# A recurrence and an MLP in one kernel: the first step's scores issued at once, ScalarE's weight passes ordered one by one, new orders of the work

## The chip, the cores and the metric

The kernel runs on one core of one Trainium2 chip. The metric is the device time of one execution in microseconds; the time before is the median of three runs.

## The reference

Two blocks are computed one after the other, in float32. The first is a gated linear recurrence over 768 positions for 4 x 8 heads of width 48; the second is a two-layer network with a PReLU between its layers, applied to the 3072 rows of 384 that the first one gives.

```python
# q, k, v, f_logit: (4, 8, 768, 48)
f = 1.0 / (1.0 + np.exp(-f_logit))
for t in range(S):
    state = f[:, :, t, :, None] * state + np.einsum('bhd,bhe->bhde', k[:, :, t], v[:, :, t])
    y[:, :, t] = np.einsum('bhd,bhde->bhe', q[:, :, t], state)
x = y.transpose(0, 2, 1, 3).reshape(B * S, H * D)          # 3072 x 384
h = x @ w_in                                               # w_in: 384 x 2048
g = np.maximum(h, 0.0) + alpha * np.minimum(h, 0.0)
out = g @ w_out                                            # w_out: 2048 x 384
```

## The kernel before

The work is cut into twelve steps: a step is a pair of batches (`bp`, 0 or 1; `u` counts the two batches in it) and a chunk of 128 positions (`c`, 0 to 5). Each step goes through four stages, each a Python generator that yields between its parts:

- `prepare` loads f, q, k and v, takes the sigmoid on ScalarE (f), copies q into `qd` and multiplies it into three lagged copies on VectorE (L275), makes running products (`ps`, `ss`, L305, L307), and from these the scaled queries `us` and `q3` and the scaled keys `k4`, `ks`, `kh`. In the first chunk of a pair of batches it also makes `k16` and `q16` (L375, L392). Its last part copies q3 into the matrix `A` on ScalarE (L407) and, for later chunks, moves the transposed keys into `ksn` by sixteen small DMAs on SP's queue (L415).
- `carry` makes the scores between blocks (`off`, L432; for the first chunk also the k16 products, L442), which ScalarE copies into `ad` (L446) and `A` (L450). For a first chunk it transposes the keys on TensorE (`pk`, L459) and ScalarE copies them to `ksn` (L462). Then it makes the products of keys and values (`pd`, L472) and moves the state on into `vs` (`moved`, L482 to L488).
- `attend` makes the scores inside blocks: `raw` from k and the lagged q (L508), `qu` from k4 and us (L523), which VectorE copies under masks into `ad` (L514; L545 in a first chunk, L529 in others), ScalarE copies `ad` into `A` (L551), TensorE multiplies by vs (`py`, L562), ScalarE copies that out (`y`, L571), and DMAs from three queues turn it into `xT` (L591). In the first step TensorE does this instead (`xt`, L580).
- `network` multiplies xT by w_in in eight tiles (`ph`, L606), ScalarE and VectorE apply the PReLU (`neg` L611, `gate` L613), and TensorE multiplies by w_out: plainly in the first step (`po`, L626), by a seven-product scheme in the others (`pa` to `pe`, L645, with sums `S` of the gates, L687, and `u2`, `o` on VectorE).

The weights come in sixteen pieces of 64-bit words. A piece is fetched into a `raw` buffer by SP (L196), ScalarE makes three passes over it (`pos` L201, `neg` L203, the low part L204) and VectorE two (`lead` L214, `both` L219). The halves of w_out are then combined on VectorE (`W`, L706).

PSUM has eight banks: four as two double banks (`pair`, for raw, qu, off, pk, pd, py) and four single ones (`bank`, for ph, po, pa to pe, xt, idle). TensorE, VectorE and ScalarE take their instructions in the order in which the program issues them, and that order is written out by hand: one string per step, in which a letter runs a stage to its next yield and a number repeats it. P and Q are `prepare` of this step and of the next, O is `carry`, S `attend`, n `network` of the step before, a and b the ScalarE passes on w_in and w_out, w and v the VectorE passes on them, W the sums of w_out.

```python
first = (
    "P5 a w P a2 O w S w a w a2 S Q S O S w Q2 S Q2 S w",
    "a2 w b w O w n2 b2 v S P v2 n2 S b v Q n b n O S2 v n b v n Q2 b v Q b n S v2 W Q W S n2 W n W",
    ...
)
usual = "S n2 O P n S Q n2 Q n3 O n S2 n Q S Q2 S n3"
```

POOL's and SP's queues are ordered by the planner of the framework. Ahead of the first step 56 small idle products run on TensorE.

Of the kernel before, what the change touches and what calls it, by code (L numbers as in the profile page):

```python
# [8 lines left out]
F32 = mybir.dt.float32  # L9
I16 = mybir.dt.int16  # L10
# [14 lines left out]
NB = DB // 4  # L25
WP = 768
IDLE = 56
RAWS, TOPS, LEADS = 4, 3, 4


@with_exitstack
def kernel(
# [62 lines left out]
    def pair(name):  # L95
        return psa.tile([128, 2, 512], F32, tag="pair", name=name)
# [71 lines left out]
    def load_weights(dst, src, name):  # L168

        rows_ = NK if dst is w_in_sb else 1  # L180
        pieces_ = dst.shape[1] * dst.shape[2] // WP
        if rows_ == 1:
            dst = dst.rearrange("p a n -> p (a n)").unsqueeze(1)
        width = WP // rows_
        words = src.rearrange("p (a n) -> p a n", a=rows_).bitcast(I16)
        got = {}

        def of(n):
            return dst[:, :, n * width:(n + 1) * width]

        def by_row(t):
            return t.rearrange("p (a n) -> p a n", a=rows_)

        def upper(n):
            raw = stage.tile([128, WP, 4], I16, tag="raw", name=f"{name}_raw{n}", bufs=RAWS)
            nc.sync.dma_start(out=raw.rearrange("p (a n) four -> p a (n four)", a=rows_)[:, :, 0:4 * width - 1],  # L196
                              in_=words[:, :, 4 * n * width + 1:4 * (n + 1) * width])

            top = raw[:, :, 2]
            pos = stage.tile([128, WP], I16, tag="pos", name=f"{name}_pos{n}", bufs=TOPS)  # L200
            nc.scalar.activation(pos, top, AF.Relu, bias=bias[:, 0:1], scale=8.0)  # L201
            neg = stage.tile([128, WP], I16, tag="wneg", name=f"{name}_neg{n}", bufs=TOPS)
            nc.scalar.activation(neg, top.bitcast(U16), AF.Relu, bias=bias[:, 1:2], scale=8.0)  # L203
            nc.scalar.activation(as_int(n, I32), by_row(raw.bitcast(U32)[:, :, 0]), AF.Copy, scale=2.0 ** -13)  # L204
            got[n] = raw, pos, neg

        def as_int(n, dtype):
            t = of(n).bitcast(dtype)
            return t if dtype is I32 else t.rearrange("p a (n two) -> p a n two", two=2)[:, :, :, 1]

        def lead(n):
            raw, pos, neg = got.pop(n)
            t = stage.tile([128, WP], BF16, tag="lead", name=f"{name}_lead{n}", bufs=LEADS)
            nc.vector.tensor_tensor(t, pos.bitcast(BF16), neg.bitcast(BF16), ALU.subtract)  # L214
            got[n] = t

        def both(n):
            t = by_row(got.pop(n).bitcast(I16))
            nc.vector.tensor_tensor(as_int(n, I16), as_int(n, I16), t, ALU.add)  # L219

        def uppers():
            for n in range(pieces_):
                upper(n)
                yield

        def rests():
            for n in range(pieces_ + 1):
                if n < pieces_:
                    lead(n)
                if n:  # L230
                    both(n - 1)
                yield

        return uppers(), rests()

    def rows(par):
        return slice(64 * par, 64 * par + D)
# [182 lines left out]
    def carry(bp, c, x):  # L420

        i = f"{bp}_{c}"
        q3, ks, kh, f64 = (x[n] for n in ("q3", "ks", "kh", "f64"))
        off = pair(f"off_{i}")
        for u in range(U):
            for hp in range(HP):
                for cc in range(NC2):
                    g = (u * HP + hp) * NC2 + cc
                    o = (u * HP + hp) * DB
                    for par in range(2):  # L430
                        r_ = rows(par)
                        nc.tensor.matmul(off[CH * cc:CH * cc + DB, par, o:o + DB],  # L432
                                         lhsT=kh[r_, g], rhs=q3[r_, g, 2], start=True, stop=True)
        if not c:
            for u in range(U):
                for hp in range(HP):
                    for j in range(NJ):
                        g = (u * HP + hp) * NJ + j
                        o = U * HP * DB + (u * HP + hp) * 16
                        for par in range(2):  # L440
                            r_ = rows(par)
                            nc.tensor.matmul(off[DB * j:DB * (j + 1), par, o:o + 16], lhsT=x["k16"][r_, g],  # L442
                                             rhs=x["q16"][r_, g], start=True, stop=True)
            for u in range(U):
                o = U * HP * DB + u * HP * 16
                nc.scalar.copy(ad[:, u, :, :, 16:DB], off[:, :, o:o + HP * 16].rearrange("p r (h t) -> p r h t", h=HP))  # L446
        for cc in range(NC2):
            s_ = slice(CH * cc, CH * cc + DB)
            for par in range(2):
                nc.scalar.copy(A[s_, :, par * HP:(par + 1) * HP, CH * cc + DB:CH * (cc + 1)],  # L450
                               off[s_, par, 0:U * HP * DB].rearrange("p (u h t) -> p u h t", u=U, h=HP))


        if not c:
            pk = pair(f"pk_{i}")
            for u in range(U):
                for hp in range(HP):
                    a = (u * HP + hp) * NC2
                    nc.tensor.transpose(pk[:, u, hp * 128:(hp + 1) * 128], ks[:, a:a + 2].rearrange("p c s t -> p (c s t)"), ident)  # L459
            ksn = x["ksn"] = work.tile([128, U, HP * 128], F32, tag="ksn", name=f"ksn_{i}", bufs=1)  # L460
            for u in range(U):
                nc.scalar.copy(ksn[:, u], pk[:, u])  # L462
        yield
        pd = pair(f"pd_{i}")
        ksn = x["ksn"]
# [28 lines left out]
    def attend(bp, c, x):  # L494

        i = f"{bp}_{c}"
        k, k4, us = (x[n] for n in ("k", "k4", "us"))


        QL, QS = (UW, UW) if c else (VW, C)  # L500
        for u in range(U):
            raw = pair(f"raw{u}_{i}")
            for hp in range(HP):
                for j in range(NJ):
                    g = (u * HP + hp) * NJ + j
                    for par in range(2):
                        r_ = rows(par)
                        nc.tensor.matmul(raw[DB * j:DB * (j + 1), par, hp * C:hp * C + QW],  # L508
                                         lhsT=k[r_, g * DB:(g + 1) * DB], rhs=qd[r_, g], start=True, stop=True)
            adu = ad[:, u].rearrange("p r h (i t) -> p (r h) i t", t=4)  # L510
            rv = raw.rearrange("p r (h x) -> p (r h) x", h=HP)
            for d in range(4):
                n = 4 - d
                nc.vector.copy_predicated(  # L514
                    adu[:, :, :, d:4], mraw[:, d, :, d:4].bitcast(I32).unsqueeze(1).broadcast_to((128, H, NB, n)),
                    rv[:, :, QO[d]:QO[d] + NB * n].rearrange("p h (i t) -> p h i t", t=n))
            qu = pair(f"qu{u}_{i}")
            for hp in range(HP):
                for j in range(NJ):
                    g = (u * HP + hp) * NJ + j  # L520
                    for par in range(2):
                        r_ = rows(par)
                        nc.tensor.matmul(qu[DB * j:DB * (j + 1), par, hp * QS + 4:hp * QS + QL],  # L523
                                         lhsT=k4[r_, g * DB:(g + 1) * DB], rhs=us[r_, g, 4:QL], start=True, stop=True)
            if c:
                for m in range(1, NB):
                    lo = UO[m] + (4 if m == 1 else 0)
# [5 lines left out]
            else:  # L533
                qv = qu.rearrange("p r (h x) -> p (r h) x", h=HP)
                adh = ad[:, u].rearrange("p r h (a t) -> p (r h) a t", a=2)
                for m in range(1, NQ):
# [5 lines left out]
                    if m > 1:  # L542
                        to = adh[:, :, :, 4 * m:16]
                        of, by = (t.rearrange("p h (a t) -> p h a t", a=2) for t in (of, by))
                    nc.vector.copy_predicated(to, by, of)  # L545
            yield

        for u in range(U):
            for j in range(NJ):
# [139 lines left out]
    def halves_of_w_out():  # L689
# [12 lines left out]
        for to, x_, y_, op in ((t3, b22, b12, ALU.subtract), (t2, t3, b11, ALU.add), (t4, t2, b21, ALU.subtract),  # L702
                               (b12, b12, b11, ALU.subtract)):
            for h in range(2):
# [3 lines left out]

    idle = bank("idle")

    steps = [(bp, c) for c in range(NC) for bp in range(B // U)]
    first = (
        "P5 a w P a2 O w S w a w a2 S Q S O S w Q2 S Q2 S w",
        "a2 w b w O w n2 b2 v S P v2 n2 S b v Q n b n O S2 v n b v n Q2 b v Q b n S v2 W Q W S n2 W n W",
        "n S P n2 S n W n O Q n3 O S Q n S Q n Q S2 Q n3",
        "S n3 P S Q S n O n O n4 Q S Q S Q n S Q n3",
    )
    usual = "S n2 O P n S Q n2 Q n3 O n S2 n Q S Q2 S n3"
    pieces = {key: part for keys, parts in (("aw", load_weights(w_in_sb, w_in, "w_in")),
                                            ("bv", load_weights(w_out_sb, w_out, "w_out")))  # L720
              for key, part in zip(keys, parts)}

    pieces["W"] = halves_of_w_out()

    def begin(n):
        if n >= len(steps):
# [72 lines left out]
```

## Time and profile before

| | |
|---|---|
| median of three runs | 626.85 us (626.29 to 627.31) |
| the profiled execution, its own time | 627.25 us |
| its span, first to last instruction | 625.4 us |
| TensorE busy | 590.1 us, 94% |
| VectorE busy | 502.5 us, 80% |
| ScalarE busy | 265.3 us, 42% |
| ph, the largest group on TensorE | 260.3 us, 1152 instructions |

A float32 product shows as two MATMUL instructions. PE is TensorE, PEld its weight load, DVE VectorE, ACT ScalarE, POOL GpSimd, SP SyncE; a q behind an engine's name is its DMA queue. L508 is line 508 of the kernel. A share of busy time is an average over the whole span; the stages at the start have other limits than the rest.

### The profile page before, as it was taken

What the parts mean: (1) busy time and instruction counts of PE and PEld (TensorE: products, weight loads), DVE (VectorE), ACT (ScalarE), POOL (GpSimd) and SP (SyncE); (2) the same over time, 40 slices, a digit from 0 to 9 for tenths busy, and PEclk for the clock granted to TensorE, in tenths of its full rate; (3) what the DMA queues carried; (4) which work ended last, traced back from release to release, by engine and by line L of the source; (5) the groups of instructions that cost most, each with busy time, mean ns of one, the idle gap of its engine ahead of it and who ended that gap; (6) DMA issues with size and microseconds to landing.
All of it is one profiled execution on the core that took longest, in us unless ns stands there. A gap on an engine that the chain in (4) does not pass through costs nothing.

```text
span 625.4 us, 19119 instructions
## 1 busy us (share of the span) xinstructions
PE 590.1 (94%) x8220; PEld 525.8 (84%) x8220; DVE 502.5 (80%) x1013; ACT 265.3 (42%) x482; POOL 60.5 (10%) x119
## 2 busy tenths in 40 slices
PE   3458999999999999999999999999999999999997
PEld 3346876789899889889889889889889889889997
DVE  7599889999799599699699699699799789663261
ACT  5797893361442542442443343353253253222110
POOL 8020001001001001001001001001001000000000
PEclk9996999999999999999999999999999999999999
DMA  9766514313414313313313223223222310300100
GB/s 314 261 229 191 176 60 95 77 35 87 85 36 91 78 37 86 65 57 85 58 64 85 54 69 85 53 69 77 59 71 68 70 37 12 66 4 12 41 0 26
DMA packets 68116, 50.43 MB, mean 81 GB/s; under 512 B 47168, under 2 KB 60608, under 8 KB 68032
## 3 DMA queue, kind: packets, MB, share of 16 engines
q1 hardware_dynamic: 56656, 25.01, 15.4%
q0 software_dynamic: 6864, 22.35, 12.7%
q10 hardware_dynamic: 4512, 1.85, 1.4%
q8 instruction: 65, 1.06, 0.7%
q14 instruction: 19, 0.16, 0.1%
HBM read 36.21 MB, written 4.72 MB: 65 GB/s over the span
## 4 chain that ended last, share of the span: by engine, by line
PE 70%; DVE 19%; ACT 8%; issue 1%; DMA 1%; ACTq 0%; DVEq 0%
PE ph L606 37%; PE pa L645 8%; PE pc L645 7%; PE pb L645 4%; PE qu L523 3%; PE pe L645 2%; PE pd L645 2%; DVE us L318 2%; PE raw L508 2%; PE py L562 1%; PE pd L472 1%; DVE q L356 1%; DVE us L309 1%; DVE k L335 1%; DVE vs L486 1%
## 5 line engine op out<-in xcount | busy, mean ns | idle before, releaser
L606 PE MATMUL ph<-xT,w_in_sb 128*128 128x256 f32 x1152 | 260.3, 384 | 0.1
L606 PEld LDWEIGHTS ph<-xT,w_in_sb 128*128 128x128 f32 x1152 | 217.6, 191 | 32.9 <-issue 2.6
L611 ACT ACTIVATE neg<-ph 128x512 f32<-128x512 f32 x96 | 57.2, 597 | 200.8 <-PE ph L606 154.1
L613 DVE SCALAR_TENSOR_TENSOR gate<-neg,om,ph 128x256 f32<-128x256 f32 x192 | 82.0, 477 | 59.7 <-ACT neg L611 59.6
L645 PE MATMUL pa<-w_out_sb,gate 128*128 128x192 f32 x352 | 63.4, 333 | 0.0
L645 PE MATMUL pc<-t,S 128*128 128x192 f32 x352 | 60.9, 326 | 0.0
L645 PEld LDWEIGHTS pa<-w_out_sb,gate 128*128 128x128 f32 x352 | 56.7, 190 | 2.1 <-DVE gate L613 0.6
L645 PEld LDWEIGHTS pc<-t,S 128*128 128x128 f32 x352 | 57.8, 190 | 0.1
L514 DVE COPY_PREDICATED ad<-mraw,raw 128x256 f32<-128x256 int32 (+1 forms) x96 | 42.4, 442 | 8.3 <-PE raw L508 5.8
L529 DVE COPY_PREDICATED ad<-mquad,qu 128x224 f32<-128x224 int32 (+6 forms) x140 | 41.9, 300 | 6.2
L551 ACT COPY A<-ad 32x256 f32<-32x256 f32 x96 | 38.6, 402 | 1.4
L571 ACT COPY y<-py 128x512 f32<-128x512 f32 x24 | 12.9, 592 | 58.1 <-PE py L562 58.1
L318 DVE TENSOR_TENSOR us<-us,fs 128x768 f32<-128x768 f32 (+5 forms) x60 | 37.0, 616 | 0.3
L302 ACT COPY us<-qd 128x256 f32<-128x256 f32 x48 | 29.8, 675 | 7.6 <-DVE qd L275 7.5
L687 DVE TENSOR_TENSOR S<-gate 128x512 f32<-128x512 f32 x44 | 30.3, 688 | 0.8
L645 PE MATMUL pb<-t,gate 128*128 128x192 f32 x176 | 30.4, 326 | 0.0
L645 PE MATMUL pe<-w_out_sb,S 128*128 128x192 f32 x176 | 30.4, 326 | 0.0
L645 PE MATMUL pd<-w_out_sb,S 128*128 128x192 f32 x176 | 30.4, 326 | 0.0
L508 PEld LDWEIGHTS raw<-qd,k 48*32 48x32 f32 x1536 | 18.3, 109 | 14.3 <-issue 8.7
L508 PE MATMUL raw<-qd,k 48*32 48x80 f32 x1536 | 23.3, 243 | 7.1 <-ACT A L450 5.2
L407 ACT COPY A<-q 48x512 f32<-48x512 f32 x44 | 27.1, 617 | 6.7 <-DVE q L356 6.1
L562 PEld LDWEIGHTS py<-A,vs 128*64 128x64 f32 x768 | 24.8, 144 | 5.8 <-issue 2.2
(109 smaller groups left out, 743.8 us busy)
## 6 DMA issues: line engine op xcount, KB each, us to landing
w_out_raw<-in_w_out SPq DMA_DIRECT2D x8, 767.8 KB, 4.5
w_in_raw<-in_w_in SPq DMA_DIRECT2D x8, 767.2 KB, 8.3
q<-in_qT POOLq DMA_DIRECT2D x11, 512.0 KB, 4.1
f<-in_fT POOLq DMA_DIRECT2D x11, 512.0 KB, 4.1
k<-in_kT POOLq DMA_DIRECT2D x11, 512.0 KB, 4.5
out<-o SPq DMA_DIRECT2D x24, 192.0 KB, 2.1
vs<-in_v POOLq DMA_DIRECT2D x22, 192.0 KB, 3.5
ksn<-kt SPq DMA_DIRECT2D x80, 32.0 KB, 2.0
```

The source lines that it names most:

```text
L302: nc.scalar.copy(q4[:, :, :, r], qdv[r][:, :, :, 0])
L318: nc.vector.tensor_tensor(us[:, :, UO[m]:UO[m] + 4 * n].rearrange("p g (i r) -> p g i r", r=4), us[:, :, skip:skip + 4 * n].rearrange("p g ...
L508: nc.tensor.matmul(raw[DB * j:DB * (j + 1), par, hp * C:hp * C + QW], lhsT=k[r_, g * DB:(g + 1) * DB], rhs=qd[r_, g], start=True, stop=True)
L514: nc.vector.copy_predicated(adu[:, :, :, d:4], mraw[:, d, :, d:4].bitcast(I32).unsqueeze(1).broadcast_to((128, H, NB, n)), rv[:, :, QO[d]: ...
L529: nc.vector.copy_predicated(ad[:, u, :, :, 4 * m:DB], mquad[:, lo:lo + n].bitcast(I32).unsqueeze(1).unsqueeze(1).broadcast_to((128, 2, HP, ...
L551: nc.scalar.copy(A[s_, u, :, s_], ad[s_, u].rearrange("p r h t -> p (r h) t"))
L562: nc.tensor.matmul(py[64 * par:64 * par + 64, u, o:o + CH], lhsT=vs[bp][:, cc, u, hd * D:hd * D + 64], rhs=A[:, u, par * HP + hp, CH * cc: ...
L606: nc.tensor.matmul(ph[:, j * T:(j + 1) * T], lhsT=w_in_sb[:, kt, m * 128:(m + 1) * 128], rhs=xT[:, kt], start=(kt == 0 and j == 0), stop=( ...
L611: nc.scalar.activation(neg, phv, AF.Relu, scale=-1.0)
L613: nc.vector.scalar_tensor_tensor(gate[:, m % NH, m // NH], neg[:, j], om[:, m:m + 1], phv[:, j], ALU.mult, ALU.add)
L645: nc.tensor.matmul(to[:, 0:DH], lhsT=of(f), rhs=by(f), start=(f == 0 and not more), stop=(f == NH - 1), skip_group_check=True)
L687: nc.vector.tensor_tensor(to, x_, y_, op)
```

## The change

Five things are changed. Three raw buffers hold the fetched pieces of weights instead of four. Each of ScalarE's three passes over a piece is now a part of its own in the order, w_in's and w_out's in one line ("a"), and the next piece is fetched after the third pass of the one whose buffer it takes. In the first step, `attend` issues the raw scores of both batches at once, before the rest of `prepare`, then both batches' masked copies and qu; `off` and `pk` of that step take single banks, and a yield divides `carry` there. In all first chunks the k16 products and their copies (four instead of two) come before those of `off`. Seven idle products of 128x256 ("J") are put into the first step's order, and all orders are new.

```diff
-RAWS, TOPS, LEADS = 4, 3, 4
+RAWS, TOPS, LEADS = 3, 3, 4
...
-        def upper(n):
-            raw = stage.tile([128, WP, 4], I16, tag="raw", ..., bufs=RAWS)
+        def fetch(n):
+            raw = raws[n] = stage.tile([128, WP, 4], I16, tag="raw", ..., bufs=RAWS)
             nc.sync.dma_start(...)
+        def upper(n):
+            top = raws[n][:, :, 2]
             pos = stage.tile(...)
             nc.scalar.activation(pos, top, AF.Relu, bias=bias[:, 0:1], scale=8.0)
+            yield
             neg = stage.tile(...)
             nc.scalar.activation(neg, top.bitcast(U16), AF.Relu, bias=bias[:, 1:2], scale=8.0)
-            nc.scalar.activation(as_int(n, I32), by_row(raw.bitcast(U32)[:, :, 0]), AF.Copy, scale=2.0 ** -13)
-            got[n] = raw, pos, neg
+            got[n] = pos, neg
+            yield
+            low = raws.pop(n).bitcast(U32)[:, :, 0]
+            nc.scalar.activation(as_int(n, I32), by_row(low), AF.Copy, scale=2.0 ** -13)
...
-        off = pair(f"off_{i}")
-        ... off products (moved behind the k16 products)
+        plain = (bp, c) == steps[0]
+        def two(name):
+            if plain:
+                return [bank(f"{name}{n}_{i}") for n in range(2)]
+            t = pair(f"{name}_{i}")
+            return [t[:, n] for n in range(2)]
+        off = two("off")
         if not c:
             ... k16 products
             for u in range(U):
-                nc.scalar.copy(ad[:, u, :, :, 16:DB], off[:, :, o:o + HP * 16]...)
+                for par in range(2):
+                    nc.scalar.copy(ad[:, u, par, :, 16:DB], off[par][:, o:o + HP * 16]...)
+        ... off products
         ... copies of off into A
+        if plain:
+            yield
         if not c:
-            pk = pair(f"pk_{i}")
+            if plain:
+                spare.clear()
+            pk = two("pk")
...
+        if (bp, c) == steps[0]:
+            raws = [scores(u) for u in range(U)]
+            yield
+            qus = []
+            for u in range(U):
+                within(u, raws[u])
+                qus.append(quad_scores(u))
+            yield
+            for u in range(U):
+                between(u, qus[u])
+            yield
+        else:
+            for u in range(U):
+                within(u, scores(u))
+                between(u, quad_scores(u))
+                yield
...
+    def kept_busy():
+        while True:
+            if not spare:
+                spare.append(bank("spare"))
+            nc.tensor.matmul(spare[0][:, 0:256], lhsT=ones[:, 0:128], rhs=ones[:, 0:256], start=True, stop=True)
+            yield
...
     first = (
-        "P5 a w P a2 O w S w a w a2 S Q S O S w Q2 S Q2 S w",
-        "a2 w b w O w n2 b2 v S P v2 n2 S b v Q n b n O S2 v n b v n Q2 b v Q b n S v2 W Q W S n2 W n W",
-        "n S P n2 S n W n O Q n3 O S Q n S Q n Q S2 Q n3",
-        "S n3 P S Q S n O n O n4 Q S Q S Q n S Q n3",
+        "P S P a P J a J2 P a J4 w a2 P w a P a O a O a S a3 w a S w S a2 Q S a3 O a S Q w a w Q S Q2",
+        "a2 w a3 n2 a O w v a4 S a2 v n S w P a3 v2 a S a n Q a v n S n O a2 n2 a v a Q a2 S Q v a4 v n v S W Q2 n2 Q W3 n",
+        "S n3 S n S n Q n W n O n S O n Q n S Q2 n S Q n2",
+        "S n P n O n S Q n3 S n Q n O S n Q n S Q2 S n Q n2",
     )
-    usual = "S n2 O P n S Q n2 Q n3 O n S2 n Q S Q2 S n3"
+    usual = "S n2 S n O n O n Q n3 Q n Q S3 n Q S n Q n Q n"
+    def uppers(parts):
+        for n in range(RAWS):
+            parts[n][0](parts[n][2])
+        for n, (_, upper, m) in enumerate(parts):
+            yield from upper(m)
+            if n + RAWS < len(parts):
+                fetch, _, ahead = parts[n + RAWS]
+                fetch(ahead)
+            yield
+    pieces = {"a": uppers(parts_in + parts_out), "w": in_rests, "v": out_rests}
+    pieces["J"] = kept_busy()
```

## The prediction

> **What bounds the kernel now.** I read the page first, then the busy time by stretch, then the timelines of ScalarE, TensorE, VectorE and the DMA queue. The page's first two parts (busy share; 40 slices, each 15.6 us):
>
> ```profile
> PE 590.1 (94%) x8220; PEld 525.8 (84%) x8220; DVE 502.5 (80%) x1013; ACT 265.3 (42%) x482; POOL 60.5 (10%) x119
> ...
> PE   3458999999999999999999999999999999999997
> ...
> ACT  5797893361442542442443343353253253222110
> ```
>
> PE is full from slice 5 on and idle for over half of slices 1 to 4, where ACT is nearly full. Busy time by stretch (PE, PEld, DVE, ACT, POOL, then clock and DMA):
>
> ```profile
> 20.00:27.70 7.70, 2.56 (x76) 2.12 (x66) 2.08 (x4) 7.66 (x14) 0.00 (x0) 1.00 0.69 197
> 27.70:38.00 10.30, 5.83 (x292) 4.99 (x293) 8.18 (x19) 10.24 (x14) 1.42 (x3) 1.00 0.72 231
> ...
> 46.00:58.00 12.00, 8.86 (x213) 7.32 (x214) 11.88 (x24) 8.05 (x13) 0.95 (x2) 0.71 0.52 147
> 58.00:66.00 8.00, 8.00 (x143) 6.60 (x145) 4.50 (x8) 5.64 (x13) 0.00 (x0) 0.79 0.59 193
> ```
>
> ACT sets 20 to 46 us, PE everything after 58. Of the 35.3 us that PE idles (625.4 - 590.1), 28 lie before 58 us; what is left is little. The timelines give the places (start, length, in brackets the idle time ahead and what ended it):
>
> ```profile
> 19.84 1.25 ACT L407 COPY A<-q 48x512 f32<-48x512 f32 x2 [6.06 <-DVE q L356]
> ...
> 45.60 1.07 ACT L571 COPY y<-py 128x512 f32<-128x512 f32 x2
> ```
> ```profile
> 27.77 1.34 PE L508 MATMUL raw<-qd,k 48*32 48x80 f32 x64 [5.22 <-ACT A L450]
> ...
> 46.82 4.51 PE L580 MATMUL xt<-y,dense 128*128 128x256 f32 x12 [2.00 <-ACT y L571]
> ...
> 55.95 1.97 PE L459 MATMUL pk<-ident,ks 128*128 128x128 f32 x8
> 57.71 7.17 PE L606 MATMUL ph<-xT,w_in_sb 128*128 128x256 f32 x24
> ...
> 119.48 1.07 PE L523 MATMUL qu<-us,k 48*32 48x112 f32 x64 [1.31 <-DVE ad L529]
> ```
> ```profile
> 251.98 1.08 PE L523 MATMUL qu<-us,k 48*32 48x112 f32 x64 [0.41 <-DVE vs L486]
> ```
> ```profile
> 110.69 3.56 DVE L706 TENSOR_TENSOR t<-t,w_out_sb 128x768 f32<-128x768 f32 x4
> 114.27 0.87 DVE L613 SCALAR_TENSOR_TENSOR gate<-neg,om,ph 128x256 f32<-128x256 f32 x2
> ```
>
> Read: ACT once idles 6.06 us; the scores wait 5.22 us for ACT; the network (ph) starts at 57.7 though its input is ready at 51.7; VectorE finishes w_out's sums at 114.3, which costs PE 1.31 us; and a 0.4 us wait recurs in the later steps.
>
> **The change, part by part.** All terms are from this execution: 625.4 us of span, 627.25 us of its own time, 0.4 above the median 626.85 (626.29 to 627.31). I subtract what is gained from the median.
>
> *Scores at once.* With off and pk in four single banks, both double banks are free for raw0 and raw1. They follow the last lagged product (9.88 + 0.61 = 10.5 us) at 2 x 1.34 and are done by 13.2, not 32.9. The masked copies still wait for the copies of off into ad (L446), now at 23.1, and then take two L514 groups of 1.88, one w round of 1.42 (L214 and L219) and two L545 groups of 1.01: done at 30.4 instead of 37.9. By itself this brings nothing, since ACT's queue is the path. L446 becomes four copies instead of two: two took 0.31, a 128x64 copy 0.14 (L304), so +0.3.
>
> *Weight passes.* One piece takes 2.56 (pos 0.91, neg 0.87, low 0.78). Before L407 ACT now fits two pieces, not one. The second piece was issued near 4.6 and landed after 9.6, at 14.2, so ACT waits 0.4 for it. L407 comes 0.47 later (one L214 now stands before VectorE's last products): 20.3. So ACT's idle time goes from 6.1 to about 3.9. From 20.3 on its queue is: L407 1.26, pos 0.89, L446 0.56, L450 1.29, neg 0.88, ksn 0.95, low 0.79, a piece 2.56, pos 0.91, A 1.66, neg and low 1.66, f/kr/qd 2.57, A 1.66, a piece 2.56, vs 0.98, pos 0.91, us 2.28, neg 0.88: 25.3, so y starts at 45.6. That is the same as before: the idle time saved has gone into two more weight passes, the later L407 and L446. py (41.5 + 3.16) is ready by then. xT is ready near 51.7, as before.
>
> *Three buffers.* Pieces 3, 4, ... are fetched after low of 0, 1, ...: at 14, 17, 27 us, needed at 27, 29.5, 38. Landings took 4.2 to 16.8; 10.9 for the one nearest in time, which I take. At 16.8 piece 3 would cost 3.8. No other queue entry stands behind these fetches on SP until xT's at 97 us.
>
> *Idle products.* Seven of 128x256, each 0.45 (5.45/12) at best and 0.75 (4.51 x 2/12) as xt ran: 3.2 to 5.3 us in PE's empty stretch 13.2 to 19.5, ahead of the k16 products that wait for VectorE (L392). Cost nothing; with that cover gone they'd cost 3.2 to 5.3. Their gain: off, k16 and pk shorter (pk 1.97), but ACT, not PE, is what those copies wait for. Zero.
> Behind an idle stretch PE is slow here: the granted clock was 0.50 from 48 to 50 us, after PE had idled 2.0 us, and py took 3.16 at 41.7 where it takes 2.0 in full work. After this change PE idles from about 31 to 41 us, so I leave py and xt at their slow 3.16 and 4.51.
> [...]
>
> *ph first.* In step 1 the network's first two tiles now precede k16, off, pk. ph starts at 51.4, ends at 56.8 (5.45; if as slow as before, 7.17: 58.5). Then k16 1.3, off 0.7, pk 1.1 (half of 1.97): 60. ACT meanwhile: five passes to 56.0, two neg, one pass, L446, L450 to 60.2, ksn to 61.2. raw0 follows the first, qu0 the second, 0.7 each: ph2 starts at about 62.0; before, the third tile started at 66.24. PE is 4.2 ahead. But ACT now holds it: 20.5 us of queue (12 weight passes 10.4, L407 1.2, eight A copies 3.3, four neg 2.0, f/kr/qd 2.6, vs 1.0) end the vs copies at 81.7, and py waits for them, while PE is there at 62.0 + 18.5 (six tiles 16.1, scores 1.4, pd 0.9) = 80.5. So po ends at 81.7 + 2.0 + 20.8 = 104.5, not 107.4: 2.9.
> VectorE, from the last gates at 85.8 (after ACT's two passes and two neg, 2.7, behind vs): three w_out rounds 4.26, one L219 0.95, scans 1.32, L309/L335/L318 3.12, moved 2.14, the two product groups 3.7 and 4.4, W 5.45, in all 25.3: 111.1, 3.2 earlier than 114.27. qu1 of step 2 waits for the masked copies behind it (4.2, to 115.3), and PE is there at 104.5 + 10.5 = 115.0: the wait of 1.31 becomes 0.3. Start-up gain: 2.9 + 1.0 = 3.9. Bounds: 0.8 (slow ph and a late landing partly) to 5.
>
> *New usual order.* From 203.72 to 250.65 a step took 46.93; all eight from 156.36 to 536.23 took 379.87, 4.4 over 8 x 46.93. Named in the waits after 140 us: qu on L486 2.0 (five times 0.4), py on A 0.3. The moved pass (L482, L486) now comes before the last product group (4.4 us), so it ends some 5 us before the next scores: 2.3 goes. What is late next: py moves ahead of pc and pd, while eight A copies come after us and kept on ACT. From the end of ph7: neg 0.55, us 1.97, kept at 2.75, copies 3.33: 6.4 us; PE after pa and pb (5.3) and half of py (1.0) is there at 6.3. So 0.1 a step, 0.8 in all. Net 1.5; bounds 4.4 and -4.
>
> **Sum:** 3.9 + 1.5 = 5.4; 626.85 - 5.4 = 621.45 us.
>
> **Rivals.** (1) *Only the start-up counts:* py's wait for A takes what qu's wait gave (0.3 a step instead of 0.1), so the order gives -0.1 and the gain is 3.8 or less: about 623.3. For it: the tie at py is worked out from rows to 0.1 us. Against: even 0.3 needs a late us copy.
> (2) *Slower: pd waits for ksn.* In the usual order O moves from after ph7 to after ph3, 15 us after the step's start instead of 26, while its operand comes through 16 DMAs issued one by one on SP:
>
> ```profile
> 203.37 0.47 SPq L621 DMA_DIRECT2D out<-o  x1
> 203.88 1.25 SPq L415 DMA_DIRECT2D ksn<-kt  x2
> 205.24 0.53 SPq L621 DMA_DIRECT2D out<-o  x1
> 205.82 7.07 SPq L415 DMA_DIRECT2D ksn<-kt  x9
> ```
>
> 16 x 0.61 = 9.8 us, plus two stores (1.0) that wait for VectorE's last sums, plus 2.0 to 3.9 to land. The transpose ends 2 us before the step's start, so the last lands at 11 to 13: 2 us to spare. If SP starts only after the second store (at 1.5), it lands at 14 to 16; a further 2 us for a landing beside the 512 KB loads makes the wait 1.5 to 3. It decides above 5.4/8 = 0.7 us a step; at 1.6 us, eight steps cost 12.8, net 12.8 - 5.4 = 7.4: 634.3.
> (3) *No change:* a piece lands at 16.8 (3.8 us of ACT) and ph runs slow (1.7), together 5.5, which eats the 5.4: 626.9. Against: less is queued ahead of piece 3 than of the one that took 16.8.
>
> **How the numbers follow.** Forecast (gain 3 to 9) 0.60, rival 1 0.14, rival 3 0.06, rival 2 and its smaller forms 0.20. A measurement can tell about 0.2% (1.25 us): faster is below 625.6, slower above 628.1. Faster 0.74, same 0.06, slower 0.20. The forecast's own range is 617.8 to 624; with rivals 1 and 3 and the mild half of rival 2 the range is 617.8 to 629.
>
> **What would show it.** Right: raw0 and raw1 before 14 us; y near 45.6; ph from 51 to 52, ahead of k16; last W pass near 111; the qu waits on L486 gone; steps of about 47.05. Wrong: y or xT several us from 45.6 and 51.7; a wait of pd on ksn's DMAs; py waiting over 0.5 us for A; ACT idle before a weight pass.

## The result and the profile after

The changed kernel takes 630.98 us (median of 7 runs, 628.64 to 631.81), the kernel before 626.36 us on the same chip (624.88 to 627.31). The ratio is 1.0061, 95% interval [1.0046, 1.0076]: slower by 4.6 us, where 5.4 us of gain were predicted, and above the range (617.8 to 629.0). The profiled execution of after took 631.81 us with a span of 630.0 us, so it is the slowest of its seven; the numbers below are of this execution.

Busy shares and the 40 slices (15.75 us each) of the page of after:

```profile
PE 593.1 (94%) x8234; PEld 529.1 (84%) x8234; DVE 503.8 (80%) x1013; ACT 261.0 (41%) x486; POOL 62.6 (10%) x119
...
PE   7337899999999999999999999999999999999997
...
ACT  6398895362352244244244244244244244223110
```

ScalarE (ACT) was nearly full in slices 2 to 4 before and has a 3 in its second slice now, in which it mostly waits. Busy time by stretch for the place (PE, PEld, DVE, ACT, POOL, then clock, DMA share, GB/s):

```profile
20.00:24.00 4.00, 0.69 (x74) 0.59 (x64) 1.98 (x5) 2.21 (x3) 0.00 (x0) 0.92 0.99 322
24.00:28.00 4.00, 0.00 (x0) 0.00 (x0) 0.00 (x0) 0.00 (x0) 0.00 (x0) 0.50 0.92 194
```

From 24 to 28 us no engine does anything; only DMAs run. The timelines of TensorE and ScalarE say who waits for whom:

```profile
10.54 2.82 PE L519 MATMUL raw<-qd,k 48*32 48x80 f32 x128 [2.23 <-ACT us L301]
13.29 4.88 PE L753 MATMUL idle<-ones 128*128 128x256 f32 x14
19.71 0.99 PE L440 MATMUL off<-us 48*32 48x16 f32 x96 [1.53 <-DVE us L391]
29.32 0.44 PE L440 MATMUL off<-us 48*32 48x16 f32 x32 [8.63 <-issue]
```
```profile
20.32 1.25 ACT L406 COPY A<-q 48x512 f32<-48x512 f32 x2 [2.46 <-DVE q L355]
21.59 0.98 ACT L202 ACTIVATE w_in_pos<-w_in_raw,bias 128x768 int16<-128x768 int16 x1
29.87 0.56 ACT L445 COPY ad<-off 128x64 f32<-128x64 f32 x4 [7.30 <-PE off L440]
```
```profile
54.04 1.07 ACT L607 COPY y<-py 128x512 f32<-128x512 f32 x2
```

The scores do run at 10.5 to 13.4 us, as predicted. But TensorE breaks off the k16 products after 96 of 128, with all operands ready, and stands 8.63 us on "issue": on nothing that the profile knows as data. ScalarE's copy L445 (L446 in the kernel before; line numbers are those of each run's own kernel) waits 7.30 us for it, and its queue stands in order behind. y starts at 54.04 us; predicted was 45.6, and 45.60 was seen before. The first scores of step 3 (counted from 0) start at 161.43 us (156.36 before): 5.1 us late, about the whole loss. The other 3.4 us of y's delay are made up in between; 1.7 of them in xt, which took 2.83 us here and 4.51 before (more on that at the end).

What came at 27.8 us? The DMA view of two adjoining stretches of after, queues by packets, MB and share (18 to 26 us, then 26 to 28):

```profile
q1 hardware_dynamic: 594, 1.18, 51.7%
q0 software_dynamic: 368, 1.29, 48.5%
```
```profile
q1 hardware_dynamic: 150, 0.28, 65.1%
q0 software_dynamic: 22, 0.05, 10.2%
q8 instruction: 1, 0.02, 4.2%
```

Queue q8 moved one 16 KB packet, from 26.48 to 27.82 us by the trace, and TensorE went on 1.5 us later. The whole run has 65 such packets, and the trace has 16,717 records of TensorE (products, weight loads and semaphore instructions): about 256 a packet. In the 19 traces of this document there are 51 places where TensorE's products stand still for more than 0.2 us on "issue". In 48 of them TensorE had just run record 449 or one that lies a multiple of 256 after it (705, 961, 1217 and so on; once one record earlier), and it went on 1.2 to 1.6 us after a packet of q8 had landed. By these counts the packets are read here as blocks of TensorE's own program. Each of the small float32 products here is 4 such records, two weight loads and two MATMULs (the 56 idle products at the start show as 224).

The kernel before has three "issue" waits in the waits view of 20 to 60 us:

```profile
PE pd L472 <- issue: 2.4, 1, 2.4
...
PE off L442 <- issue: 1.3, 1, 1.3
...
PE raw L508 <- issue: 0.6, 1, 0.6
```

Those of off and raw are of the same kind: they come after records 1729 and 961 and end 1.4 us after a packet. The largest, pd's, is not. It comes after record 1144, and it is one of the three exceptions (the others are pd's in runs 4 and 7, which start from the kernel before). By the trace a semaphore instruction of TensorE lasts from 34.10 to 36.88 us there, and VectorE's masked copies of raw end just before, at 36.84:

```profile
34.99 1.85 DVE L514 COPY_PREDICATED ad<-mraw,raw 128x256 f32<-128x256 int32 x4
```

So pd waited for VectorE, although the view says "issue".

In the kernel before the 705th record came at 28.3 us, and the block had landed at 23.8, while TensorE waited 5.22 us for ScalarE anyway. The change issues the raw scores of both batches (256 records) and seven idle products (28) ahead of k16, so TensorE used up its stock at 20.5 us.

### The profile page after: what moved, and what is told of

The parts are those of the page before. It is cut to its first block, busy times and chain, and to the rows that moved or that the text cites. A ratio compares the mean times of both kernels' runs of the same rounds, so it can differ in the third digit from the quotient of the medians.

```text
span 630.0 us, 19144 instructions
## 1 busy us (share of the span) xinstructions
PE 593.1 (94%) x8234; PEld 529.1 (84%) x8234; DVE 503.8 (80%) x1013; ACT 261.0 (41%) x486; POOL 62.6 (10%) x119
## 4 chain that ended last, share of the span: by engine, by line
PE 58%; DVE 18%; ACT 15%; issue 6%; DMA 1%; SPq 0%; ACTq 0%; DVEq 0%
PE ph L642 23%; PE pc L681 9%; PE pa L681 6%; PE pd L681 5%; PE pe L681 4%; ACT A L587 4%; DVE gate L649 3%; DVE S L723 3%; PE qu L540 3%; ACT us L301 3%; PE raw L519 2%; DVE qd L274 2%; PE py L598 2%; ACT neg L647 2%; PE pb L681 2%
## 5 line engine op out<-in xcount | busy, mean ns | idle before, releaser
L681 PE MATMUL pa<-w_out_sb,gate 128*128 128x192 f32 x352 | 61.2, 327 | 0.0
L528 DVE COPY_PREDICATED ad<-mraw,raw 128x256 f32<-128x256 int32 (+1 forms) x96 | 42.2, 442 | 13.1 <-ACT ad L445 8.2
L598 PE MATMUL py<-A,vs 128*64 128x64 f32 x768 | 28.6, 232 | 12.5 <-ACT vs L499 9.7
L699 ACT COPY o<-pa 128x192 f32<-128x192 f32 x11 | 3.5, 318 | 78.4 <-PE pa L681 68.5
L274 DVE TENSOR_TENSOR qd<-qd,f 128x768 f32<-128x768 f32 (+2 forms) x36 | 27.6, 766 | 3.0 <-ACT qd L269 3.0
L681 PEld LDWEIGHTS pe<-w_out_sb,S 128*128 128x128 f32 x176 | 28.9, 190 | 0.0
```

Source lines behind the costliest of these rows:

```text
L274: nc.vector.tensor_tensor(qdv[d], qdv[d - 1][:, :, :, 1:5 - d], f[:, :, 1:5 - d].rearrange("p (g i) r -> p g i r", i=NB), ALU.mult)
L528: nc.vector.copy_predicated(adu[:, :, :, d:4], mraw[:, d, :, d:4].bitcast(I32).unsqueeze(1).broadcast_to((128, H, NB, n)), rv[:, :, QO[d]: ...
L598: nc.tensor.matmul(py[64 * par:64 * par + 64, u, o:o + CH], lhsT=vs[bp][:, cc, u, hd * D:hd * D + 64], rhs=A[:, u, par * HP + hp, CH * cc: ...
L681: nc.tensor.matmul(to[:, 0:DH], lhsT=of(f), rhs=by(f), start=(f == 0 and not more), stop=(f == NH - 1), skip_group_check=True)
```

## Experiments

Theory F: the loss is TensorE's wait for its second block, and where it falls is set by the count of instructions ahead of it. Rivals: B, three buffers or the new order of weight passes hold ScalarE; O, the new orders themselves are worse; S, the k16 products wait for data or a bank that the profile does not name. "Dry" below means that TensorE stands on "issue" at record 449 or a multiple of 256 after it, with what q8 had brought by that count used up; "after" is the changed kernel. Ratios are to the kernel before, with their 95% intervals; runs without one are single executions.

**1. No small idle products.** The kernel starts with 56 products of 128x32x8 that nobody reads (224 records), before and after alike.

```
-IDLE = 56
+IDLE = 0
```

> The changed kernel without the 56 small idle products ahead of the first step (224 TensorE instructions fewer; the seven large ones stay). Theory F (TensorE ran out of fetched instructions after about 705 of them at 20.7 us and waited until the next 16 KB block, queued behind weights and inputs, had come at 27.8): the k16 and off products and pk now fit into what is fetched (about 684 instructions), L445 starts near 22.5 instead of 29.9, the wait moves into qu and is at most 3 us long, y starts between 45.5 and 48.5 instead of 54.0, time 622 to 625. Theory S (a hidden wait for data or a bank in the k16 products): the wait of 8.6 us stays in the middle of the k16 products, time about 631. Theory O (the new orders are themselves slower): the wait goes but the time stays above 627.

Measured 624.1 us, 0.9965 [0.9951, 0.9979]. TensorE's timeline of this run:

```profile
19.64 1.25 PE L440 MATMUL off<-us 48*32 48x16 f32 x128 [2.06 <-DVE us L391]
22.88 1.18 PE L453 MATMUL off<-q,kh 48*32 48x32 f32 x64 [1.99 <-ACT ad L445]
24.00 1.97 PE L472 MATMUL pk<-ident,ks 128*128 128x128 f32 x8
25.89 0.40 PE L540 MATMUL qu<-us,k 48*32 48x52 f32 x8
27.52 1.74 PE L540 MATMUL qu<-us,k 48*32 48x52 f32 x120 [1.22 <-issue]
```

k16 runs in one piece, L445 starts at 22.42 us, y at 46.57. The dry place is still record 705, now 8 products into qu, and costs 1.22 us. Taking useless work away turned a loss of 4.6 us into a gain of 2.4, and time, y and the new place of the wait came as F said. The wait is no longer in the k16 products, as S would have it, and the new orders are all still there, so O does not explain the loss either.

**2. 40 idle products**, to move the dry place by 64 records only.

> The changed kernel with 40 instead of 56 small idle products: 64 TensorE instructions fewer, just the 64 that are left of the k16 products when TensorE stands still. Theory F: the place of the wait moves by 64 instructions: all 128 k16 MATMULs run by 21.2, L445 starts near 22.5, and TensorE stands still at the start of off (L453) until 27 to 30; L458 then waits instead of L445, so the time is within 2 us of the changed kernel. Theory S: 96 k16 MATMULs and then the wait, as in the changed kernel.

```profile
19.92 1.25 PE L440 MATMUL off<-us 48*32 48x16 f32 x128 [1.96 <-DVE us L391]
28.31 1.08 PE L453 MATMUL off<-q,kh 48*32 48x32 f32 x64 [7.14 <-issue]
```

630.05 us in one execution. The wait moved behind the last k16 product, to the same place in the count (704 records).

**3. Four buffers** (`RAWS = 4`, IDLE 56).

> The changed kernel with four raw buffers again: piece 3 is fetched at the start and not at 15 us. Theory F1 (the block of instructions comes late because piece 3 now moves between 18 and 28 us): the block arrives near 23.8 as in the kernel before, the wait in the k16 products is 4 to 5 us instead of 8.6, time 627 to 628. Theory F2 (pieces 4 and 5 move up in its place, so just as much stands ahead of the block): the wait stays between 7 and 10 us, time 630 to 632. Theory S: the same as F2.

630.54 us, 1.0067 [1.0045, 1.0089]. The wait is 6.71 us, between the two forms of F in the text (F1: 4 to 5 us, F2: 7 to 10); the time is the changed kernel's. Three buffers are not the cause, so the first half of rival B falls. Its other half, the order of the weight passes, is the same in run 1, where the loss is gone.

**4. Late orders only**: the kernel before with the changed orders of the third, fourth and usual steps.

> The kernel before with the new orders from the third step on (third, fourth and usual string; the second string gets one more Q, as the new ones have that part a step earlier), nothing else changed. Prediction's term: 1.5 us faster (bounds 4.4 and -4). By the steps of the changed kernel, which took 379.2 us for eight against 379.9: 0.7 faster, 625.5 to 626. Rival: the loss of the changed kernel sits here: 628 or more.

626.96 us, 1.0005 [0.9993, 1.0018]. In the profile eight steps took 378.46 us instead of 379.87, but the times show neither a gain nor the loss of rival O.

**5. Copies apart.** After has waits inside a tile besides: the lagged products of off (L453) wait for the copies L445 out of the same bank (1.99 us in run 1), and in step 1 the second half of pk waits for the first ksn copy out of the same pair. (The change also puts each ksn copy right behind its own four transposes; in the kernel before both copies follow all eight.) In the timeline of after:

```profile
68.00 1.11 PE L472 MATMUL pk<-ident,ks 128*128 128x128 f32 x4 [1.39 <-ACT ksn L473]
```

The edit, with IDLE = 0: all products of off ahead of the copies L445, and all transposes ahead of the first ksn copy (shortened):

```
         k16 products (L440)
-        copies ad<-off (L445)
         lagged products (L453)
+        copies ad<-off
...
         transposes of u = 0, 1
+        for u in range(U):
             nc.scalar.copy(ksn[:, u], pk[u])
```

> The changed kernel without the small idle products and with two orders inside carry put back: all off products ahead of the copies of k16's scores (L445), and all eight transposes (pk) ahead of both ksn copies. Theory W (the second loss is in waits that the change adds inside a tile: off on L445 2.0 and 0.8 us, A on off 1.2 and 0.9, pk's second half on the first ksn copy 1.4): these waits go, the vs copies of step 1 end 2 to 3 us earlier than 83.5, time 621 to 622.8. Rival V (VectorE's chain of w_out sums sets the end anyway): the waits go, the last W pass stays where it is, time 623.8 to 624.6.

621.86 us, 0.9933 [0.9915, 0.995]: faster than both kernels, by 4.2 us than before. Two of its lines, from ScalarE's and VectorE's timelines:

```profile
45.53 1.07 ACT L609 COPY y<-py 128x512 f32<-128x512 f32 x2
```
```profile
105.61 3.55 DVE L744 TENSOR_TENSOR t<-t,w_out_sb 128x768 f32<-128x768 f32 x4
```

y is where the prediction had it, the vs copies of step 1 end at 79.8 us and step 3 starts at 150.49. TensorE is still dry in qu (3.07 us) and pd (2.51), where ScalarE has other work in its queue, and in step 1 in raw (0.72) and ph (1.50).

**6 to 8.** After without idle products of either kind; the kernel before with IDLE = 0; and the first scores issued after k16 and off (`"P2 a P J a ... O S a O ..."`).

> The changed kernel without any idle products, small or large. Theory F with the prediction's term (the large ones lie in TensorE's empty stretch and what they warm is not on the path): the same as without the small ones alone, 623.4 to 624.8, k16, off and pk no slower than 1.25, 1.18 and 1.97. Rival (the large ones raise the clock for the first step): slower by 1 us or more, 625 and up.

625.3 us, 0.9986 [0.9972, 1.0]: a miss, 1.2 us slower than run 1, in the range of the text's rival. k16 took 1.44 us instead of 1.25; off (1.19) and pk (1.97) were as in run 1, and so was L445's start to 0.1 us. What the large products bring stays open here; run 12 asks again.

> The kernel before without its 56 small idle products, as a control. Theory F: its own waits for instructions (2.4 us before pd, 1.3 us in the second k16 products) move or shrink, but 5 us of its start are set by ScalarE and VectorE: 625 to 627. Rival (the small idle products cost time in any kernel): 624.5 or less.

626.52 us, 1.0 [0.9986, 1.0015]: without the change the small products neither help nor hurt.

> The changed kernel with one part undone: the first step's raw scores are issued after the k16 and off products (small and large idle products stay). Theory F: 256 instructions fewer stand ahead of k16, so k16 and off run without a wait and L445 starts near 22.5; TensorE runs dry in the raw scores instead, after about 705 instructions, until 26 to 28 us, and the masked copies start near 28 to 29: y at 47 to 50, time 625 to 628. Theory S (a wait of the k16 products for something of their own): the wait of 8 us stays in them, 630 or more.

629.77 us, 1.007 [1.0046, 1.0093]. The place came as F said, the size did not: k16 ran without a break (L445 at 22.53 us) and TensorE was dry in raw, for 2.90 us, but the transposes of pk queue in order behind the scores (29.44), so the ksn copies waited 4.12 us and y came at 51.15.

**9. Weight fetches put off** (pieces 3 and 4 fetched later in the order).

> The changed kernel with the fetches of pieces 3 and 4 put off until after the third piece's passes, so that up to 1.5 MB of weights less move between 15 and 27 us; all instructions of TensorE stay. A probe of the wait, not of the time: piece 3 itself may come late. Theory Q (the block of instructions stands behind weights and inputs): it arrives by 18 to 23 us instead of 26.5 to 27.8 and the wait in the k16 products falls from 8.6 to 4 us or less. Theory R (the block comes when it comes, whatever else moves): block from 25 us on, wait 7 us or more.

629.57 us, wait 6.7 us. The probe failed: SP issued the fetches as early as before (3.63 MB from 14 to 28 us, 3.60 in after), so it tells nothing on the traffic.

**10 to 12. Copies apart with one thing put back or taken away**: IDLE = 56; four buffers; no large idle products.

> The version with the two orders inside carry put back (621.9 us), but with the 56 small idle products of the changed kernel. If the two losses add (small idle products 6.9 us, from 631.0 to 624.1; orders inside carry 2.2, from 624.1 to 621.9): 628 to 629.5. Rival: with the off products ahead of the copies, the wait for instructions covers both, and the orders inside the first step bring nothing: 630 or more.

628.02 us, 1.0025 [1.0009, 1.0041], wait 6.4 us: the 224 records of useless products cost 6.2 us here.

> The version with the two orders inside carry put back and no small idle products (621.9), with four raw buffers. Prediction's view (three buffers cost nothing, since no landing is waited for): 621 to 622.8. Rival (the block of instructions or a piece comes earlier with four): 620.8 or less.

621.91 us, 0.992 [0.990, 0.9941].

> The same version (621.9) without the seven large idle products too. Prediction's view (they bring nothing): 621 to 622.8. Rival from the run without any idle products, which was 1.2 us above the one without the small ones: 623 or more.

622.09 us, 0.993 [0.991, 0.995]. The fourth buffer changes nothing. The seven large products are worth 0.2 us here, within the noise, and 1.2 us by runs 1 and 6, so at most a little.

**13 to 16. Why is the block so late?** It may stand behind the bulk loads (DMA share 0.9 to 1.0 in that stretch) or be asked for late. Four single executions of after with other traffic. Runs 13 and 15 hold back loads of the second step (13 all four, 15 q, f and k) until L445, by a small copy on GpSimd; run 14 adds two loads; run 16 holds back w_in's pieces 3 to 5 too.

```
+            if (bp, c) == steps[1]:                      # runs 15, 16: into the tile that is loaded
+                nc.gpsimd.tensor_copy(t[:, 0:1], ad[:, 0, 0, 0, 16:17])
```

> The changed kernel, with the second step's four loads (q, f, k, v: 1.9 MB, issued at 14.2 to 17.7 us in the changed kernel) held back until the lagged scores are copied (L445) by one small copy on GpSimd. If the instruction block waits behind the bulk loads: it lands well before 25.9 us, at 16 to 22, and TensorE's wait in the lagged products falls from 8.6 to under 3 us. If it comes at a time of its own: it lands at 25.9 to 27.8 and the wait stays at 6.4 to 8.6. The whole time says little, since the second step's inputs come later.

> The changed kernel with two more loads of 524 KB each (nobody reads them) ahead of the second step's loads on GpSimd's queue. If the block waits behind the bulk loads: 1.05 MB at the stretch's 390 GB/s is 2.7 us, so it lands 2 to 3 us later, near 29 to 31, with a wait of 10 to 12. If it comes at a time of its own: 25.9 to 27.8, wait 6.4 to 8.6.

> The changed kernel, with the second step's loads of q, f and k (1.6 MB) held back until the lagged scores are copied (L445), by small copies on GpSimd into the first column of their tiles. If the instruction block is late because the DMA engines are full: from about 20 us on they are idle, the block lands at 16 to 22 us, and TensorE's wait in the lagged products falls under 3 us. If it comes at a time of its own: it lands at 23.5 to 27.8 as in the other runs, and the wait stays at 5 to 8.6 us. The whole time says little, since the second step's inputs come later.

> As the run before (the second step's q, f and k held back until the lagged scores are copied, L445), and w_in's pieces 3, 4 and 5 held back in the same way, so that bulk loads end near 16 us. If the instruction block is late because the DMA engines are full: it lands by 19 us, TensorE never stands in the lagged products, and L445 starts near 22.5. If it comes at a time of its own: it lands at 22 us or later and the wait stays at 3 us or more. The whole time says nothing, since ScalarE then waits for its weight pieces.

Run 13 failed as a probe: the copy was placed behind the loads, which went out at 14.2 us as in after; the block came at 23.95 to 25.24, wait 5.89. Run 14: block at 23.48, wait 5.07, not later with 1.05 MB more; the bulk loads went on past 30 us, the third and fourth blocks came late (30.70 and 36.58), and TensorE was dry twice more (2.66 and 2.99 us). Run 15: block at 22.34, wait 3.97; between the two expectations (under 3, and 5 to 8.6). Run 16 says most. Busy time by stretch, and TensorE's timeline:

```profile
18.00:20.00 2.00, 1.81 (x38) 1.19 (x37) 2.00 (x5) 0.08 (x1) 0.00 (x0) 1.00 0.00 0
20.00:22.00 2.00, 0.76 (x91) 0.66 (x67) 1.96 (x5) 1.57 (x3) 0.00 (x0) 1.00 0.03 8
```
```profile
19.78 0.99 PE L444 MATMUL off<-us 48*32 48x16 f32 x96 [0.19 <-DVE us L395]
23.36 0.44 PE L444 MATMUL off<-us 48*32 48x16 f32 x32 [2.60 <-issue]
```

The DMA engines were empty from 18 us (share 0.00), yet the block moved only from 21.05 to 22.01, after TensorE had run dry. Neither theory is whole: full DMA engines are not needed for the block to be late, by 2.60 us here. In none of the 19 traces does a block begin to move while more than 298 records are left before the place that needs it; just when it does is less clear. The 513th record, the start of k16, came at 19.77, and the block began to move 1.28 us later; from there to dry are 192 records, which k16 uses up in 0.8 us. What asks for a block is not shown, and record 513 is no rule: in the kernel before, the block ahead of this one moved at 10.2 us, while the record 256 earlier, 257, ran only at 17.8.

The loads seem to add to the wait. From record 513 to the block it took 1.28 us with no bulk data moved, 2.63 with 0.78 MB (run 15), and 3.7 to 6.8 us in after and runs 3, 9, 10, 13 and 14, with all loads (6.78 in after, with 1.93 MB; 3.66 in run 14, which has more to load). How much a given load adds stays open: runs of the same traffic as after gave waits of 5.9 to 8.6 us.

**17. 32 more idle products** (`IDLE = 88`), so that record 513 falls into the scores at 13 us.

> The changed kernel with 88 small idle products at the start instead of 56: 128 instructions more, nothing else changed. If the supply of instructions is the cause: instruction 513 now starts during the scores (near 13 us), the second block lands by 20 us, all 128 k16 products run at once and L445 starts near 22.5 us instead of 29.9; the third block is asked for near 20.3 and TensorE stands, if at all, in the lagged products of off after its 961st instruction, for 1 to 4 us. y starts at 47 to 50 us instead of 54.0, and the time is 626 to 628.5 us, although work was added. If the cause were anything else in the change (fewer buffers, the new orders, the idle products' own time): the wait before L445 stays at 6 to 9 us and the time at 630 to 632.

632.83 us, 1.0107 [1.0086, 1.0128]. The first part came as expected, the time did not. TensorE's timeline:

```profile
19.71 1.25 PE L440 MATMUL off<-us 48*32 48x16 f32 x128 [0.47 <-DVE us L391]
22.95 0.56 PE L453 MATMUL off<-q,kh 48*32 48x32 f32 x32 [1.99 <-ACT ad L445]
26.62 0.65 PE L453 MATMUL off<-q,kh 48*32 48x32 f32 x32 [3.10 <-issue]
...
50.99 4.85 PE L616 MATMUL xt<-y,dense 128*128 128x256 f32 x12 [1.61 <-ACT y L607]
...
65.76 0.43 PE L453 MATMUL off<-q,kh 48*32 48x32 f32 x14 [2.09 <-issue]
```

The block moved at 14.38, k16 ran whole, L445 started at 22.48, the dry place is record 961 (3.10 us) and y came at 49.77: 4.3 us ahead of after. That is given back in step 1: xt took 4.85 us instead of 2.83 (2.0; the mean granted clock was 0.58 over it, 1.00 in after), off is dry again for 2.09 at record 1985 and qu for 0.80, so the second scores start at 76.74 us, 1.1 later than in after. The expectation followed only one block; all of them had moved. Moving a dry place is not removing it.

## Why the prediction was wrong

The step that failed is the start-up gain of 3.9 us, and in it the paragraph "Scores at once". It let ScalarE's queue run from 20.3 us without a wait, since L446's operands would be there: "ACT's queue is the path". With TensorE's supply short, L445 waited 7.30 us, L458 behind it 1.17 more for the products of off, and y came 8.4 us late. At step 3's start the prediction had 3.9 us of gain and the run 5.1 of loss, so 9.0 us are missing, and 8.4 of them are there at y. The prediction counted the durations of what moves ahead of k16 (2 x 1.34 us of scores, idle products that "cost nothing" in an empty stretch) and never its instructions. Runs 1 and 10 show what a count can cost: 224 records of the smallest products are worth 6.2 to 6.9 us when they stand ahead of this place, and nothing in the kernel before (run 7). The "issue" waits of before, of which two (0.6 and 1.3 us) were for instructions, were in the waits view and were passed over. (The text of run 7 counts pd's 2.4 us among them; as shown above, pd waited for VectorE.)

*Rivals.* None named it. Rival 2, which had all of the 0.20 given to "slower", did not occur: pd does not wait for ksn in the later steps. Rival 3 looked at ScalarE's late weight piece; it waits 1.35 us once, at 12.6 us, and nothing follows from it.

*Signs.* "y or xT several us from 45.6 and 51.7" was given as the first mark of a wrong prediction, and it is what the profile shows.

*Right, once the supply is out of the way* (run 5): y at 45.53 (45.6), vs copies at 79.8 (81.7), last sum of w_out at 109.2 (111.1), raw0 and raw1 by 13.1 us. The start-up gain there is 5.9 us by step 3's start (3.9 said; xt's 1.7 us is in it). The whole gain, 4.2 us, is close to the 5.4 of the sum, in part by luck: run 5 also leaves out the small idle products and changes two orders, and a larger start-up gain stands beside a usual order that brings almost nothing. Three buffers cost nothing, as said (run 11); that the seven large products bring nothing is borne out by run 12 (0.2 us) but not by run 6 (1.2).

*Terms mis-sized.* (a) The "k16 1.3, off 0.7, pk 1.1" of step 1 have waits between them that the sum left out, 0.81 for L445 and 1.39 for ksn, 2.2 us, because products and copies now alternate in one tile; run 5 against run 1 gives 2.2 us for these and the like waits of the first step. (b) "New usual order" 1.5 us: the qu waits are gone as said, but eight steps took 379.17 us against 379.87, and the tie at py is nearer rival 1's 0.3 than 0.1. The prediction's own terms for it (0.55, 2.75 and 3.33) add up to 6.6 us, not 6.4, which against TensorE's 6.3 is 0.3 a step. The weight loads of py in the waits of 160 to 560 us (total, times, longest):

```profile
PEld py L598 <- ACT A L587: 1.9, 7, 0.3
```

Run 4, the orders alone, gives no measurable gain. (c) xt ran in 2.83 us, not the 4.51 that was kept. This goes with the granted clock: it was 1.00 throughout xt in the nine traces with 2.83 us, and 0.50 for part or all of it in the ten with 4.2 to 5.5 (mean 0.62 in before, 1.00 in after). The idle products do not decide it: run 17 has them and took 4.85, run 7 has none and took 2.83. So a difference of 1.7 us in one profile can be xt alone. (d) The reading that PE idles for over half of slices 1 to 4 is too much: it idles 28 of the first 58 us, and no term rests on it.

## What to carry to other kernels

When work is moved ahead of a critical burst on TensorE, count its instructions as well as its time, four for each small float32 product here, and look in the kernel before for "issue" waits: 48 of the 51 over 0.2 us here mark where the supply ran out. Check each against the instruction queue's packets first, since pd's 2.4 us did not. Dummy products in an idle stretch are not free if they eat the stock before a burst: 56 small ones cost 6.2 to 6.9 us here (runs 10 and 1), and nothing in the kernel before (run 7). When one dry place is moved, follow the next ones too (run 17 had y 4.3 us earlier and still took 632.83 us), and keep products and the copies that read them from alternating in one tile (2.2 us here, run 5 against run 1).

## What the runs showed of the hardware

- Queue q8, which the page lists as "instruction", moved 65 packets of 16 KB in after, against 16,717 records of TensorE, 257 a packet. TensorE stopped after records 449, 705, 961, 1217, 1729, 1985 and others a multiple of 256 apart, in 48 of the 51 stops on "issue" over 0.2 us in the 19 traces.
- At these stops TensorE went on 1.2 to 1.6 us after a packet had landed (27.82 to 29.32 in after, 22.01 to 23.36 in run 16).
- With the DMA engines empty (share 0.00 from 18 to 20 us) the block was still late by 2.60 us in a burst of small products (run 16); with all loads moving (share 0.99 and 0.92 from 20 to 28 us in after), in the same burst, by 5.07 to 8.63 us (after, runs 3, 9, 10, 13 and 14).
- No block began to move more than 298 records before it was needed, in any of the 19 traces. In the kernel before TensorE idled for 9.29 us up to 17.59 us, and one packet of q8 moved in that time (10.23 to 11.32). What asks for a block is not shown.
- A wait that the profile gives to "issue" can also be one on a semaphore: pd's 2.4 us in the kernel before, where a semaphore instruction of TensorE lasted from 34.10 to 36.88 us.
